# RetNet attention followed by a gated MLP on one core: the third group's two chunks taken jointly, the decay tables loaded at the start, one conversion step moved

## The chip, the cores and the metric

The kernel runs on one core of one Trainium2 chip. The metric is the device time of one execution in microseconds (us). TensorE does the matrix products; VectorE (DVE in the profile), ScalarE (ACT), GpSimd (POOL) and SyncE (SP) are the other engines. Each engine takes its instructions strictly in the order in which the program wrote them down. Transfers between HBM and SBUF are issued by an engine's instruction (here nearly all by SP and by POOL) and are carried by 16 shared DMA engines; SP's transfers go through one queue (q1 in the profile), POOL's through another (q0).

## The reference, cut to what matters

The first half is a linear attention with a decay per head, for 4 batches, 8 heads, 768 positions and a head dimension of 64. The second half takes its output as 3072 tokens of 512 features and sends them through a gated MLP with 2048 hidden units.

```python
for t in range(S):
    state = gamma[None, :, None, None] * state + np.einsum('bhd,bhe->bhde', k[:, :, t], v[:, :, t])
    y[:, :, t] = scale * np.einsum('bhd,bhde->bhe', q[:, :, t], state)
...
x = np.ascontiguousarray(attn_out.transpose(0, 2, 1, 3)).reshape(B * S, H * D)
h = x @ w_in
sp = np.maximum(h, 0.0) + np.log1p(np.exp(-np.abs(h)))
g = h * erf(sp)
return (g @ w_out).astype(np.float32)
```

The two weight matrices arrive as 64-bit floats, which the kernel turns into 32-bit ones by operations on their bits.

## The kernel before, in words

**Tiling.** The sequence is cut into chunks of 128 positions (`C`), 6 to a batch, 24 in all. Two chunks make a group of 256 tokens (`GT`), 12 groups in all. Chunks 0 to 3 (groups 0 and 1) are computed at the start by functions that take a whole chunk at once. From chunk 4 on a chunk is computed in two halves of 64 positions: `begin` makes the scores and the sums for the state on TensorE (lines 566 and 573), `states` masks the scores and adds up the running state on VectorE (582, 593), `results` makes the outputs on TensorE and copies them out on ScalarE (611, 622, 630), and `crossed_sums` adds the part that belongs to the other half (641). Before that a chunk needs its transposes, `T` = `ret_transpose` (453 on TensorE, the copies at 459 on ScalarE), and its scaled inputs, `scale_early` (line 746, eight small ScalarE operations each for the queries, argument 1, and for the values, argument 0).

**The first block.** After chunk 3 the loop over `ft` = 0 to 15 computes the hidden columns of groups 0 and 1, 128 columns a step, by plain 32-bit products (`hidden_of`, line 665). Each step has this order: the products of column tile `ft`; the weight conversions that are still wanted for a later tile (`need`); the entries of the table `during` for this `ft`; then `put_hidden(ft)`, which copies the finished tile out of PSUM on ScalarE (673) and stores it with two DMAs issued by POOL (675). There are two PSUM buffers for column tiles, so the products of tile `ft + 2` wait for the copy of tile `ft`. The table `during` is where the third group, chunks a = 4 and b = 5, is worked in between the column tiles. After the block the other groups run in periods of 8 units (`unit`, `pair_unit`) on split operands, and at the end the second MLP product follows.

**What sets the order of the work around the change.** It is all written out by hand: the list of calls ahead of the block, the table `during`, and the program's order on each queue. Nothing is planned by a scheduler. Four things lie on the queues that the change touches:

- `load(4)`, `load(5)` and their values (lines 136 and 143) are issued by SP, each when the conversion of weight piece 0 or 1 is done; SP's queue also carries the weight pieces (line 195) and the many small loads `kb` and `qb` (159).
- `load_pair(6)` is stepped by the `pair` entries of `during`. Its first step, at `ft` = 2, issues four transfers of 256 KB on POOL, the values and keys of chunks 6 and 7 (lines 143 and 153).
- `load_block_scales` issues 20 small transfers on POOL (by_b at line 389, four; kq_b at line 395, sixteen). They fill tables that `block_scales` (lines 401 to 405) reads at `ft` = 6 and that `prepare` needs from `ft` = 11.
- `next(weight_steps)` runs one step of the weight conversion, here of piece 0 (lines 230 to 265, VectorE with one ScalarE operation). `A` = `ret_add` adds a chunk's sums to the state on VectorE (525) and copies half of the outputs on ScalarE (518).

Of the kernel before, what the change touches and what calls it, by code (L numbers as in the profile page):

```python
# [32 lines left out]
def head(u, r):  # L33
    return u // 2 + u % 2 * 4 + 2 * r
# [15 lines left out]
def kernel(  # L50
# [34 lines left out]
    ps_r = ctx.enter_context(tc.tile_pool(name="ps_r", bufs=2, space=PSUM))  # L85
# [59 lines left out]
    def load_pair(j):  # L145

        b, c = divmod(j, NC)
        KNP[j] = b4("kn", [2, H, D])
        KB[j], QB[j] = (b4(name, [HP, 2 * C]) for name in ("kb", "qb"))
        for i in range(2):  # L150
            load_values(j + i, nc.gpsimd)
            KN[j + i], SLOT[j + i] = KNP[j][:, i], head
            nc.gpsimd.dma_start(KN[j + i], of_chunk(k, j + i))
        yield
        for to, src in ((KB[j], k), (QB[j], q)):
            for s, d in itertools.product(range(2), range(2)):
                part = slice((2 * s + d) * 32, (2 * s + d + 1) * 32)
                for u in range(HP):
                    nc.sync.dma_start(
                        to[part, u].rearrange("p (a d) -> p a d", d=32),  # L160
                        src[b, head(u, s), c * C : (c + 2) * C, d * 32 : (d + 1) * 32].rearrange(
                            "(a p) d -> p a d", p=32
                        ),
                    )
                yield
# [111 lines left out]
    def weights():  # L277

        parts = [(n, part) for n in range(2 * NPC) for part in (range(2) if n in HALVES else (None,))]
        for i, (n, part) in enumerate(parts):  # L280
            if n >= NPC or i < 3:
                exponents(n, part)
                yield
            yield from conversion(n, part, parts[i + 1] if i > 1 and i + 1 < EARLY else ())

    weight_steps = weights()
# [76 lines left out]
    def query_scale(c):  # L363
        nc.vector.reciprocal(kq_s[:, c, 1], kq_s[:, c, 0])
        nc.vector.tensor_scalar(kq_s[:, c, 1], kq_s[:, c, 1], unscale, None, op0=ALU.mult)
# [14 lines left out]
    def other_scales():  # L380
        query_scale(slice(2, NC))
# [5 lines left out]
    def load_block_scales():  # L387
        for s, i in itertools.product(range(2), range(2)):
            nc.gpsimd.dma_start(
                by_b[s * D : (s + 1) * D, 1, 2 * i : 2 * i + 2], decay_s[i * D : (i + 1) * D, s::2]  # L390
            )
        for s, d in itertools.product(range(2), range(2)):
            part = slice((2 * s + d) * 32, (2 * s + d + 1) * 32)
            for u in range(HP):
                nc.gpsimd.dma_start(
                    kq_b[part, 0, u, 0],
                    decay_k[:, head(u, s) : head(u, s) + 1].rearrange("(a p) h -> p (a h)", p=32),
                )
# [313 lines left out]
    def pair_unit(g, ft):  # L712
# [23 lines left out]
    Q_, V_, T, S_, M, O_, A = (  # L736
        scale_q, scale_v, ret_transpose, ret_scores, ret_mask, ret_out, ret_add
    )
# [3 lines left out]
    def scale_early(j, i):  # L742
        q = QN[j].rearrange("p (c g) d -> p c g d", c=2)
        for h in range(H):
            by, x = kq_s[:, j % NC, i, h : h + 1], q[:, h % 2, h // 2] if i else V[j][:, h]
            nc.scalar.activation(x, x, AF.Copy, scale=by)
# [5 lines left out]
    keep_warm(2)  # L752
    Q_(1)
    other_scales()
    S_(0)
    T(1, 0)
    T(1, 1)
# [13 lines left out]
    M(2)  # L771
    next(weight_steps)
    O_(1)
    next(weight_steps)
    T(3, 1)
    T(3, 0)
    scale_early(2, 0)
    A(1)
    next(weight_steps)
    O_(2, partial(S_, 3))  # L780
    M(3)
# [10 lines left out]
    def steps(s, n=1):  # L792
# [3 lines left out]
    pair = load_pair(JPC + 2)  # L796
    prep = prepare(JPC + 2)
    a, b = JPC, JPC + 1
    during = {
        1: [(load_block_scales,)],  # L800
        2: [(scale_early, a, 1), (steps, pair, 2)],
        3: [(scale_early, a, 0), (T, a, None, ("o2", "o3")), (steps, pair, 2)],
        4: [(begin, a, ps_r), (steps, pair, 2)],
        5: [(scale_early, b, 1), (states, a), (steps, pair, 2)],
        6: [(scale_early, b, 0), (results, a, ("o0", "o1")), (T, b, None, ("o2", "o3")), (steps, pair), (block_scales,)],
        7: [(crossed_sums, a), (begin, b, ps_r), (split_weights, 0)],
        8: [(states, b), (split_weights, 1)],
        9: [(results, b, ("o0", "o1"))],
        10: [(crossed_sums, b), (split_x, a, 2)],
        11: [(steps, prep, 3)],  # L810
        12: [(split_weights, 2), (steps, prep, 1)],
        13: [(steps, prep, 1)],
# [187 lines left out]
    for g in range(G2, NG + 1):  # L1000
        pair = load_pair(2 * g + 4) if 2 * g + 4 < NJ else iter(())
# [85 lines left out]
```

## Time and profile before

| | us |
|---|---|
| median of 3 runs | 612.78 |
| lowest and highest of them | 612.72, 613.2 |
| the profiled execution's own time | 613.15 |
| its span | 611.4 |
| TensorE busy in the span | 604.6 |
| VectorE, ScalarE, POOL busy | 459.8, 390.3, 132.5 |

How to read it: times in the trace count from the start of the span. Every answer groups instructions by the line of the kernel that wrote them. A row of the timeline gives the start, the length, the engine, the line, the operation and its tiles, and how many instructions were merged; in brackets stands the idle time of the engine ahead of it and what ended that. The engine's name with a q (SPq) marks the instruction that issues a transfer, not the transfer. The row of DMA in the page gives the share of the 16 DMA engines that was busy, in tenths, for 40 equal slices of the span. The chain is the run of work that ended last, followed back from the end. TensorE's granted clock is 1.0 in the whole span.

### The profile page before, as it was taken

To read this page: it belongs to the slowest core of one execution; us is meant where nothing else is said; L and a number is where in the kernel's file an instruction comes from. 1 tells how busy PE (TensorE), PEld (TensorE's weight loads), DVE (VectorE), ACT (ScalarE), POOL (GpSimd) and SP (SyncE) were. 2 spreads that over 40 slices of the span, in tenths; PEclk is the share of its full clock that TensorE was granted. 3 is DMA by queue.
4 is the path that set the end of the run, shared out by engine and by line. 5 is a ranking of instruction groups with operands and counts; after the bars stand their busy time and mean duration, and the time that the engine had idled before them with its cause. 6 is when DMAs were issued, how large, how long until landed. Compare 5 with 4: busy or idle time off the path is not lost.

```text
span 611.4 us, 13214 instructions
## 1 busy us (share of the span) xinstructions
PE 604.6 (99%) x5222; PEld 507.3 (83%) x5222; DVE 459.8 (75%) x581; ACT 390.3 (64%) x614; POOL 132.5 (22%) x228
## 2 busy tenths in 40 slices
PE   8999999999999999999999999999999999999997
PEld 7888889888888888888788988888888888888886
DVE  5899988886978679787768978686776768668640
ACT  3667446354453634345387699889789888988920
POOL 1087435443526535241112200000000000000000
PEclk9999999999999999999999999999999999999999
DMA  9999659977979998894645834325324333531300
GB/s 203 312 263 281 149 132 248 265 161 221 219 201 277 269 270 182 243 233 151 215 143 187 286 119 148 127 70 173 103 88 154 106 129 110 172 119 55 103 35 34
DMA packets 143949, 106.28 MB, mean 174 GB/s; under 512 B 103056, under 2 KB 123792, under 8 KB 143888
## 3 DMA queue, kind: packets, MB, share of 16 engines
q1 hardware_dynamic: 128160, 58.09, 37.4%
q0 software_dynamic: 15168, 47.21, 24.6%
q8 instruction: 41, 0.67, 0.5%
q10 hardware_dynamic: 560, 0.14, 0.1%
q14 instruction: 20, 0.16, 0.1%
HBM read 69.75 MB, written 35.65 MB: 172 GB/s over the span
## 4 chain that ended last, share of the span: by engine, by line
PE 96%; SPq 2%; DMA 1%; ACT 0%; DVE 0%; issue 0%; DVEq 0%
PE o L720 31%; PE o L905 21%; PE r L905 11%; PE hp L905 11%; PE hp L665 9%; PE o L693 3%; PE hp L566 1%; DMA raw<-in_moe_w_in_dram 1%; PE hp L720 1%; PE r L720 1%; PE r L566 1%; PE r L611 1%; SPq L136 1%; PE r L622 1%; PE r L573 1%; PE hp L611 1%
## 5 line engine op out<-in xcount | busy, mean ns | idle before, releaser
L720 PE MATMUL o<-x_hi,w_hi 128*128 128x512 f32 x272 | 108.0, 397 | 0.0
L322 ACT ACTIVATE h<-o 128x512 f32<-128x512 f32 x74 | 43.8, 595 | 98.7 <-PE o L720 89.3
L720 PE MATMUL o<-x_lo,w_lo 128*128 128x512 f32 x272 | 106.0, 390 | 0.0
L860 DVE TENSOR_TENSOR e<-hid,e 128x1024 f32<-128x1024 f32 x48 | 56.7, 1222 | 61.9 <-ACT e L850 61.9
L323 DVE SCALAR_TENSOR_TENSOR h<-o,h 128x512 f32<-128x512 f32 x74 | 50.5, 686 | 34.3 <-ACT h L322 24.8
L720 PE MATMUL o<-x_dif,w_dif 128*128 128x512 f32 x272 | 72.7, 389 | 0.0
L731 POOL DMA_DIRECT2D hids<-h x72 | 39.6, 550 | 131.2 <-DVE h L323 123.1
L316 DVE SCALAR_TENSOR_TENSOR g_dif<-g_hi,g_lo 128x1024 fp32r<-128x1024 f32 x48 | 58.8, 1226 | 3.3
L720 PEld LDWEIGHTS o<-x_hi,w_hi 128*128 128x128 f32 x272 | 51.0, 188 | 11.4
L720 PEld LDWEIGHTS o<-x_dif,w_dif 128*128 128x128 f32 x272 | 51.1, 188 | 10.6
L314 ACT ACTIVATE g_hi<-e 128x1024 fp32r<-128x1024 f32 x48 | 51.0, 1062 | 13.5 <-DVE e L860 11.6
L720 PEld LDWEIGHTS o<-x_lo,w_lo 128*128 128x128 f32 x272 | 51.1, 188 | 10.1
L315 DVE TENSOR_TENSOR g_lo<-e,g_hi 128x1024 fp32r<-128x1024 f32 x48 | 58.6, 1221 | 0.5
L665 PE MATMUL hp<-xT,w 128*128 128x256 f32 x256 | 57.2, 381 | 0.0
L665 PEld LDWEIGHTS hp<-xT,w 128*128 128x128 f32 x256 | 48.0, 190 | 6.6
L846 ACT ACTIVATE e<-hid 128x1024 f32<-128x1024 f32 x48 | 48.2, 1052 | 0.3
L850 ACT ACTIVATE e<-e 128x1024 f32<-128x1024 f32 x48 | 48.2, 1052 | 0.3
L905 PE MATMUL o<-w_hi,g_hi 128*128 128x512 f32 x120 | 46.7, 389 | 0.0
L905 PE MATMUL o<-w_lo,g_lo 128*128 128x512 f32 x120 | 46.7, 389 | 0.0
L905 PE MATMUL o<-w_dif,g_dif 128*128 128x512 f32 x120 | 46.7, 389 | 0.0
L550 ACT ACTIVATE v<-v,kq_s 128x64 f32<-128x64 f32 x144 | 35.6, 335 | 0.0
L846 ACT ACT_TABLE_LOAD x24 | 30.8, 1283 | 0.5
(201 smaller groups left out, 1265.6 us busy)
## 6 DMA issues: line engine op xcount, KB each, us to landing
hids<-h POOLq DMA_DIRECT2D x72, 256.0 KB, 4.1
hid<-hids SPq DMA_DIRECT2D x36, 512.0 KB, 4.6
raw<-in_moe_w_in_dram SPq DMA_DIRECT2D x32, 256.0 KB, 5.5
raw<-in_moe_w_out_dram POOLq DMA_DIRECT2D x32, 256.0 KB, 6.2
hid<-hid SPq DMA_DIRECT2D x12, 512.0 KB, 5.2
out_dram<-y SPq DMA_DIRECT2D x23, 256.0 KB, 2.1
kb<-in_k_dram SPq DMA_DIRECT2D x144, 32.0 KB, 2.8
v<-in_v_dram POOLq DMA_DIRECT2D x18, 256.0 KB, 6.0
```

The source lines that it names most:

```text
L314: nc.scalar.activation(hi, x, AF.Copy, scale=KEEP)
L315: nc.vector.tensor_tensor(lo, x, hi.bitcast(F32), op=ALU.subtract)
L316: nc.vector.scalar_tensor_tensor(dif, hi.bitcast(F32), Z, lo.bitcast(F32), op0=ALU.mult, op1=ALU.subtract)
L322: nc.scalar.activation(to, a, AF.Copy, scale=1 + 1 / Z)
L323: nc.vector.scalar_tensor_tensor(to, b, -1 / Z, to, op0=ALU.mult, op1=ALU.add)
L665: nc.tensor.matmul(HP_[ft][:, g], w[:, kk, ft % 2 * P : (ft % 2 + 1) * P], XC[g][:, kk], start=(kk == 0), stop=(kk == n_k - 1),)
L720: nc.tensor.matmul(to, W[n][i][:, kk * 2 * P + u * P : kk * 2 * P + (u + 1) * P], XR[i][:, at, kk], start=(kk == 0 and i == parts[0]), sto ...
L731: nc.gpsimd.dma_start(HID2[g][:, ft % 8], h)
L846: nc.scalar.activation(E[n], HID_[n], AF.Softplus)
L850: nc.scalar.activation(E[n], E[n], AF.Erf)
L860: nc.vector.tensor_tensor(E[n], HID_.pop(n), E[n], op=ALU.mult)
L905: nc.tensor.matmul(Y[g][t][x // 2], G[n][x][:, f, t * P : (t + 1) * P], W_OUT[ft // 2][x][:, ft % 2 * d_model : (ft % 2 + 1) * d_model], s ...
```

## The change

Three edits, all to the order of calls:

1. `load_block_scales()` leaves the table entry for `ft` = 1 and is called ahead of the first scores, right after `other_scales()`.
2. The second `next(weight_steps)` of the chunks' list moves from ahead of the transposes of chunk 3 to behind `A(1)`, the addition of chunk 1's sums to the state.
3. In `during`, the chunks a = 4 and b = 5 were staggered: a's `begin`, `states`, `results` stood at `ft` = 4, 5, 6 and b's at 7, 8, 9, with b's transposes at 6. Now b's scaling stands one step earlier (4 and 5), its transposes at 5 in the PSUM tiles o0 and o1, both `begin` at 6 (b's in o2 and o3), `states` at 7 and 8, both `results` at 9 and both `crossed_sums` at 10.

```diff
@@ the list of calls ahead of the block
     Q_(1)
     other_scales()
+    load_block_scales()
     S_(0)
...
     O_(1)
-    next(weight_steps)
     T(3, 1)
     T(3, 0)
     scale_early(2, 0)
     A(1)
+    next(weight_steps)
     next(weight_steps)
@@ the table during
-        1: [(load_block_scales,)],
         2: [(scale_early, a, 1), (steps, pair, 2)],
         3: [(scale_early, a, 0), (T, a, None, ("o2", "o3")), (steps, pair, 2)],
-        4: [(begin, a, ps_r), (steps, pair, 2)],
-        5: [(scale_early, b, 1), (states, a), (steps, pair, 2)],
-        6: [(scale_early, b, 0), (results, a, ("o0", "o1")), (T, b, None, ("o2", "o3")), (steps, pair), (block_scales,)],
-        7: [(crossed_sums, a), (begin, b, ps_r), (split_weights, 0)],
+        4: [(scale_early, b, 1), (steps, pair, 2)],
+        5: [(scale_early, b, 0), (T, b, None, ("o0", "o1")), (steps, pair, 2)],
+        6: [(begin, a, ps_r), (begin, b, None, ("o2", "o3")), (steps, pair), (block_scales,)],
+        7: [(states, a), (split_weights, 0)],
         8: [(states, b), (split_weights, 1)],
-        9: [(results, b, ("o0", "o1"))],
-        10: [(crossed_sums, b), (split_x, a, 2)],
+        9: [(results, a, ("o0", "o1")), (results, b)],
+        10: [(crossed_sums, a), (crossed_sums, b), (split_x, a, 2)],
```

The number and the shapes of all operations stay as they were.

## The prediction

> **What bounds the kernel now.** I read the page first, then TensorE's waits, then the chain and the queues' timelines between 30 and 60 us, and last the two transfer queues in two windows of ten microseconds. From the page:
>
> ```profile
> PE 604.6 (99%) x5222; PEld 507.3 (83%) x5222; DVE 459.8 (75%) x581; ACT 390.3 (64%) x614; POOL 132.5 (22%) x228
> DMA  9999659977979998894645834325324333531300
> ```
>
> TensorE is busy for 604.6 of 611.4 us, so a microsecond in which it newly waits is a microsecond on the end. The second line says that the 16 DMA engines are full in the first four slices, 0 to 61 us: exactly where the change lies. TensorE's waits in the whole span have four rows, 2.9 us together; one matters here:
>
> ```profile
> PE o L497 <- ACT kqT L459: 0.6, 1, 0.6
> ```
>
> So the most that ending waits can give is 0.6 us behind the start. The chain through the first block (start, length, what):
>
> ```profile
> 38.55 0.87 PE o L453 x8
> 39.42 3.46 PE hp L665 x16
> 42.88 0.62 PE r L566 x32
> 43.97 7.11 PE hp L665 x32
> ...
> 52.16 1.02 PE o L453 x8
> ...
> 84.48 0.47 PE o L566 x32
> ```
>
> A column tile is 16 products in 3.46 us. Two of them behind a run of small products take 7.11, not 6.92. A `begin` that follows a column tile starts with 0.62, one that follows another `begin` with 0.47. Changing between the kinds of product costs something.
>
> Now the queues: POOL, then SP (issues), then ScalarE.
>
> ```profile
> 32.09 2.39 POOL L389 DMA_DIRECT2D by_b<-decay_s_dram  x4
> 45.84 1.27 POOL L675 DMA_DIRECT2D hid<-h  x2
> 47.10 0.91 POOL L143 DMA_DIRECT2D v<-in_v_dram  x1
> ...
> 36.88 0.99 SPq L136 DMA_DIRECT2D kq<-in_q_dram  x2
> 37.91 1.06 SPq L136 DMA_DIRECT2D kq<-in_k_dram  x2
> 39.01 2.61 SPq L143 DMA_DIRECT2D v<-in_v_dram  x1
> ...
> 31.86 0.56 ACT L673 COPY h<-hp 128x512 f32<-128x512 f32 x1
> 47.53 2.01 ACT L746 ACTIVATE kq<-kq,kq_s 128x64 f32<-128x64 f32 x8
> ```
>
> The 20 table transfers hold POOL from 32.09 to 45.84, 13.7 us. Behind them stand tile 1's two stores, although ScalarE had copied that tile by 32.42, and then the four 256 KB loads for chunks 6 and 7. The SP rows are chunk 5's queries, keys and values. Last, what the two queues carried in 48 to 58 us, when POOL's stores and four loads were in flight, and in 34.6 to 44.6 us, when they were not:
>
> ```profile
> q0 software_dynamic: 513, 1.52, 61.5%
> q1 hardware_dynamic: 1871, 1.13, 47.6%
> ...
> q1 hardware_dynamic: 4880, 2.22, 98.7%
> q0 software_dynamic: 505, 0.12, 6.6%
> ```
>
> (packets, MB, share). With POOL's burst in flight SP's queue moved 1.13 MB in ten microseconds, without it 2.22.
>
> **The change part by part.**
>
> The conversion step behind the addition. At 17.32 and 17.78 VectorE runs the step's two operations (0.42 and 0.69 us); the addition follows at 18.39, and TensorE's line 497 starts at 18.95. With the addition first it ends near 17.8, and line 497 can start at 18.35, when the transposes ahead of it end. But the scores behind it (465, at 19.55) need ScalarE's copy, which ends at 19.40 as before. So 0.1 us is gained of at most 0.6; I take 0.1. The step itself still ends near 20.1, and its product starts at 22.18: covered by 2 us.
>
> The tables at the start. POOL is free from 6.69 (end of line 378) to 30.84, so 13.7 us of issuing costs no engine time. The transfers now share full DMA engines with chunks 2 and 3 and the first weight piece. They are 10 KB together; with the stores of tile 0 they made the 6.6% in the last window, at most 0.66 us. About half of them would go ahead of the last loads that TensorE waits for (chunk 3's keys, near 17.9). Between 0 and 0.66 us I take 0.1, nearest to their share of the bytes. At `ft` = 6 the tables' readers wait less (0.67 us on VectorE), which TensorE does not see.
>
> The chunks jointly. One `begin` and one `results` lose their own edges: the start of `begin` 0.62 - 0.47 = 0.15, the column tile behind it 7.11 - 6.92 = 0.19, the start of `results` 0.15 (line 611 has the same 0.62), and b's transposes, now behind a column tile, 1.02 - 0.87 = 0.15. Together -0.64 us. The moved VectorE work is covered: `states` of b ends at 60.9 in the trace and both `results` are wanted near 63; both `crossed_sums` stand at `ft` = 10, and their reader, the first unit, starts at 90.94.
>
> What POOL does with the free time is the large term. Its next entries move forward to where ScalarE releases them: tile 1's stores from 45.84 to 32.4, the four loads from 47.10 to about 33.7, all by 13.4 us. So the burst of 48 to 58 comes to 34.6 to 44.6, the time in which SP's queue brings chunk 5. SP then carries 2.22 - 1.13 = 1.09 MB less, and at 0.222 MB per us it needs 1.09 / 0.222 = 4.9 us more. Queries of chunk 5 landed 5.6 us after their issue, the second at 37.37 + 5.6 = 43.0; keys 5.9 after, at 44.4; values 6.5 after, at 45.5. They come to 47.9, 49.3 and 50.4.
>
> Edit 3 wants them sooner: b's transposes started at 52.16, 7.8 us behind the keys. Now they start at 38.55 + 0.87 + 2 x 3.46 = 46.34, and tile 6 should start at 47.2. ScalarE stands at `scale_early(b, 1)` until 47.9, works 2.0 us, and behind it in its queue waits the copy of tile 4 (0.57), which frees the buffer that tile 6 writes: 47.9 + 0.1 + 2.0 + 0.6 = 50.6. TensorE waits 50.6 - 47.2 = 3.4 us, first for the keys (49.3), then for the scaled queries and the buffer. Nothing later takes it back, since TensorE has no other wait to absorb it. Next in line is tile 7, which needs tile 5's copy: ScalarE's 50.6 + 1.15 (an exponent step) + 2.0 + 1.04 + 0.57 = 55.4 against TensorE's 50.6 + 3.46 + 1.56 = 55.6; just in time. The bounds: no stall if the delay is under 1.5 us; at the other end a weight transfer issued at 49.2, inside the burst, took 11.2 us where the median is 5.4: a delay of 5.8 and a stall of 4.3. The windows stand between; I take 3.4.
>
> The sum: -0.1 + 0.1 - 0.64 + 3.4 = +2.8 us on the profiled execution's 613.15 us (span and what lies around it), 615.9. That execution lies 0.37 above the median of 612.78, so on the median's scale the forecast is 615.6.
>
> The Trainium skill, "DMA: Bandwidth & Descriptors", section "Queues, rings and completion order", says that a DMA engine takes turns between its queues by whole packets. By strict turns one of POOL's packets would pass for each of SP's; the window has 513 against 1871, so the trace does not bear that out, at least as its packets are counted; the sum by the rule is the last rival below.
>
> **The rivals.**
>
> *The loads stay hidden.* If the DMA engines take the early burst in the pauses that the sharing leaves, chunk 5 is late by under 1.5 us and the edges alone remain: -0.64, so 612.1. For it: the engines were at about 0.85 from 38 to 40 us. Against it: they are at nine tenths elsewhere, and 1.4 MB more does not fit.
>
> *Half hidden.* A delay between 1.5 and 3.3 us gives a stall of 0 to 1.8: 612.1 to 613.9, in the middle 613.0. For it: without 256-byte packets in the way SP's queue may regain more than 0.222 MB per us.
>
> *The other side: the addition sets the pace.* If line 497 was held by the addition alone and what follows it runs 0.6 us sooner all the way, and no load is late, the time is 613.15 - 0.64 - 0.63 - 0.37 = 611.5. It decides if chunk 5's keys land by 46.3. Against it: the scores' copy ends at 19.40 whatever VectorE does.
>
> *The stall grows.* A long wait could lower TensorE's granted clock, 1.0 in every slice before; half a tile's time to a whole tile's at half speed costs 1.7 to 3.5 us, 617.3 to 619.1. Or SP's queue gets only packet for packet: 513 of its packets of 0.6 KB are 0.31 MB, 1.91 MB less, 8.6 us of delay, a stall of 7.1, and 619.2. Against the first: the wait is broken by the keys' transposes after 3 us. The Trainium skill, "TensorE: Matmul & The Clock Gate", section "What's actually happening", puts the fall to half clock at an idle window of about 3.4 us; no run here shows it. The second of these is what the rule of turns would do.
>
> **How the numbers follow.** The late chunk 5 as worked out: 0.57, by itself 614.2 to 616.5 (stall 2.0 to 4.3). Hidden 0.15, half hidden 0.14, faster 0.06, grown 0.08. A measurement of this kernel can tell about 0.2%, 1.2 us. Faster is the third rival, 0.06; the same are the first two, 0.29; slower is the rest, 0.65. The range leaves out the third rival's time and the grown stalls, 0.14 together, and reaches from just under the hidden case to above the likeliest one's 616.5: 612.0 to 617.0.
>
> **What would show it.** Right: POOL's loads of chunks 6 and 7 at about 33.7; chunk 5's transfers landing about ten microseconds after their issue; ScalarE idle ahead of line 746; TensorE waits of some 3 us in all ahead of lines 453 and 665 between 46 and 51; 0.62 then 0.47 in one run of `begin`; line 497 near 18.35. Wrong: POOL's loads still after 45, or no TensorE row over 1 us in that stretch, or new waits elsewhere (at the start, on the first weight piece, or at 63 on `states`).

## The result and the profile after

The changed kernel took 615.88 us (median of six, 615.51 to 616.88) against 612.82 of the kernel before in the same comparison (612.63 to 613.2). The ratio is 1.0052, with a 95% interval of 1.0039 to 1.0065: slower by 3.1 us, where 2.8 was forecast (615.6 on the median's scale). The profiled execution of the changed kernel is its slowest, 616.88 us with a span of 615.2.

First the waits of TensorE in the kernel after (who waited for what, us in total, times, longest):

```profile
PE o L453 <- DMA kq<-in_k_dram: 2.2, 1, 2.2
PE o L417 <- POOL ident masks.py:199: 1.5, 1, 1.5
```

The 2.2 us are new: the transposes wait for keys. No other row is above 0.3 us; the 0.6 at line 497 is gone. The timeline of TensorE shows the place, and that of ScalarE, POOL and SP the causes (start, length, engine, line; the idle time ahead in brackets):

```profile
39.95 7.07 PE L665 MATMUL hp<-xT,w 128*128 128x256 f32 x32
49.27 1.55 PE L453 MATMUL o<-ident,kq 128*128 128x128 f32 x8 [2.24 <-DMA kq<-in_k_dram]
50.95 3.72 PE L665 MATMUL hp<-xT,w 128*128 128x256 f32 x16
```

```profile
48.06 0.35 ACT L746 ACTIVATE kq<-kq,kq_s 128x64 f32<-128x64 f32 x1 [3.49 <-DMA kq<-in_q_dram]
48.65 1.78 ACT L746 ACTIVATE kq<-kq,kq_s 128x64 f32<-128x64 f32 x7 [0.25 <-DMA kq<-in_q_dram]
50.34 0.56 ACT L673 COPY h<-hp 128x512 f32<-128x512 f32 x1
```

```profile
33.42 1.07 POOL L675 DMA_DIRECT2D hid<-h  x2 [0.77 <-ACT h L673]
34.48 0.91 POOL L143 DMA_DIRECT2D v<-in_v_dram  x1
```

```profile
37.69 1.19 SPq L136 DMA_DIRECT2D kq<-in_q_dram  x2
38.93 3.60 SPq L136 DMA_DIRECT2D kq<-in_k_dram  x2
```

POOL's first 256 KB load starts at 34.48 instead of 47.10. Chunk 5's queries, issued at 37.69, let ScalarE start only at 48.06, after an idle time of 3.49 us; the copy of tile 4 stands behind that scaling, and tile 6 starts at 50.95. The transfer queues in the same ten microseconds as in the prediction, 34.6 to 44.6 us (packets, MB, share of 16 engines; then issues, KB each, us to landing):

```profile
q0 software_dynamic: 519, 1.60, 55.6%
q1 hardware_dynamic: 1948, 1.35, 50.5%
...
kq<-in_q_dram SPq DMA_DIRECT2D x2, 128.0 KB, 10.3
kq<-in_k_dram SPq DMA_DIRECT2D x2, 128.0 KB, 9.0
```

SP's queue moved 1.35 MB where it moved 2.22 before, and the queries took 10.3 us from issue to landing instead of 5.6.

To see where the time went, I cut every span in three: up to the first column tile's products, from there to the first unit (the block), and the rest.

| run | change against the kernel before | first tile at | block | rest | median, and ratio with interval |
|---|---|---|---|---|---|
| before | | 22.18 | 68.69 | 520.53 | 612.79 to 612.96 in the four comparisons |
| after | all three edits | 22.88 | 71.34 | 520.98 | 615.88, 1.0052 (1.0039 to 1.0065) |
| e1 | edits 2 and 3, tables back at `ft` = 1 | 22.09 | 68.49 | 520.72 | 613.14, 1.0003 (0.9994 to 1.0012) |
| e2 | edit 1 alone | 22.84 | 68.68 | 520.68 | 613.99, 1.0018 (1.0009 to 1.0027) |
| e3 | edit 2 alone | 21.90 | 68.69 | 520.71 | 612.96, 1.0002 (0.9993 to 1.0011) |
| e4 | all, the pair's loads held | 23.18 | 68.02 | 520.60 | 613.35, 1.0008 (1.0000 to 1.0017) |
| e5 | edits 2 and 3, tables spread, loads held | 21.99 | 68.91 | 520.50 | 612.95, 1.0003 (0.9994 to 1.0012) |
| e6 | all, half of the pair's loads held | 22.92 | 68.02 | 520.56 | 613.30, 1.0009 (1.0000 to 1.0017) |
| e7 | before, 20 other transfers at the start | 21.83 | 68.68 | 520.49 | 613.02, 1.0004 (0.9995 to 1.0012) |
| e8 | all, joint chunks one tile later | 22.93 | 68.79 | 520.58 | 613.92, 1.0020 (1.0011 to 1.0029) |
| e9 | edits 2 and 3, tables by copies, loads held | 22.17 | 68.02 | 520.61 | 612.29, 0.9987 (0.9978 to 0.9995) |
| e10 | all, tables by copies | 22.30 | 72.45 | 520.75 | 617.03, 1.0054 (1.0040 to 1.0068) |
| e11 | as e10, one of four loads held | 22.09 | 69.65 | 520.66 | 614.21, 1.0020 (1.0011 to 1.0028) |

The first three columns are one profiled execution each. The rest scatters over 0.5 us, so no effect of the change can be told behind the first 95 us. The 3.8 us between the two profiled spans are 0.7 at the start, 2.65 in the block and 0.45 in the rest, which is scatter.

### The profile page after: what moved, and what is told of

The parts are those of the page before. It is cut to its first block, busy times and chain, and to the rows that moved or that the text cites. A ratio compares the mean times of both kernels' runs of the same rounds, so it can differ in the third digit from the quotient of the medians.

```text
span 615.2 us, 13216 instructions
## 1 busy us (share of the span) xinstructions
PE 606.5 (99%) x5222; PEld 508.7 (83%) x5222; DVE 459.9 (75%) x581; ACT 390.9 (64%) x614; POOL 132.9 (22%) x228
## 4 chain that ended last, share of the span: by engine, by line
PE 91%; DMA 5%; SPq 3%; DVE 1%; ACT 0%; issue 0%; DVEq 0%
PE o L720 31%; PE o L905 21%; PE hp L905 11%; PE r L905 11%; PE hp L665 6%; DMA raw<-in_moe_w_in_dram 3%; PE o L693 3%; DMA kq<-in_q_dram 2%; SPq L136 1%; PE hp L566 1%; PE r L611 1%; PE hp L720 1%; PE r L720 1%; PE r L622 1%; SPq L195 1%; PE r L566 1%
## 5 line engine op out<-in xcount | busy, mean ns | idle before, releaser
L323 DVE SCALAR_TENSOR_TENSOR h<-o,h 128x512 f32<-128x512 f32 x74 | 50.6, 687 | 35.1 <-ACT h L322 27.6
```

The lines of the kernel that those rows point to most:

```text
L323: nc.vector.scalar_tensor_tensor(to, b, -1 / Z, to, op0=ALU.mult, op1=ALU.add)
```

## The experiments

### e1: the tables back at their old place

```diff
     other_scales()
-    load_block_scales()
     S_(0)
...
+        1: [(load_block_scales,)],
         2: [(scale_early, a, 1), (steps, pair, 2)],
```

> The changed kernel with the table loads put back to ft = 1, so that POOL's stores of tile 1 and its four 256 KB loads wait behind them again. The joint taking of the chunks and the moved conversion step stay. My theory (the early burst on POOL's queue makes chunk 5 late): no TensorE wait at b's transposes, chunk 5's queries land under 6 us after their issue, and the saved edges alone remain, about 612.2 us. Rival 1 (the joint order by itself wants chunk 5 too early): the wait of 2 to 3 us at b's transposes stays and the time is 615 to 616 us. Rival 2 (the tables at the start delay everything that follows): the first column tile starts near 22.2 instead of 22.9 us and 0.7 us of the loss goes away through that alone.

The stall at b's transposes is gone: the joint order alone is not too early, and rival 1 falls. But the time is 613.14, not 612.2. The block is 68.49, and its chain (start, length) shows another wait:

```profile
48.00 1.68 ACT v L746 x7
49.73 0.21 POOL hid L675
49.94 0.82 issue
50.76 8.39 DMA hid<-h
59.25 0.60 ACT h L673
59.89 3.72 PE hp L665 x16
```

ScalarE's tile copy at 59.25 waits for a store on POOL's queue to land; the copies go through six buffers, and these are taken as long as the stores are not done. That store stood behind the table loads and the pair's four loads until 49.73, and then took 8.39 us to land, with those four loads in flight. In the kernel before that wait existed too (2.59 us on ScalarE at 58.93) and TensorE did not see it. With the joint order the products come sooner and it does: 0.20 us of waiting, and the three column tiles from 52.51 on take 11.03 us where they take 10.56 in a run without the wait (e9), which is the block's whole loss against 68.02. So the first edit is not idle: it takes this wait away, at a price of its own. How much of the wait the table loads make alone, with the pair's loads held and the tables left at `ft` = 1, was not run.

### e2: the tables at the start, nothing else

```diff
     other_scales()
+    load_block_scales()
     S_(0)
...
-        1: [(load_block_scales,)],
```

> The kernel before with the table loads at the start and nothing else changed; the staggered chunks stay. My theory: chunk 5 lands about ten microseconds after its issue, as in the changed kernel, but b's transposes are wanted only near 52 us, so TensorE does not wait: 612.8 us, within 0.6. Rival 1 (the early tables themselves cost time at the start): first column tile 0.7 us later, 613.5 us. Rival 2 (the late loads stall the block in any order): a TensorE wait over 1 us between 45 and 60 us and 614 us or more.

The block is unchanged, 68.68 against 68.69: chunk 5's queries landed 9.8 us after their issue, nearly as late as in the changed kernel, but with the staggered chunks that cost TensorE nothing. But the first tile starts at 22.84, 0.66 us later than in the kernel before, and the time is 613.99, 1.05 us above it: rival 1 holds, and my theory of "no cost" falls. The waits of TensorE name the place:

```profile
PE r L453 <- DMA kq<-in_k_dram: 0.8, 2, 0.6
```

The keys of chunk 3 are late. The five runs with the table loads at the start all have this wait, 0.2 to 1.2 us, and the eight others have none. In 7 to 17 us SP's queue moved 2.17 MB instead of 2.30.

### e3: the conversion step alone

```diff
     O_(1)
-    next(weight_steps)
     T(3, 1)
...
     A(1)
+    next(weight_steps)
     next(weight_steps)
```

> The kernel before with the second conversion step moved behind the addition of chunk 1 and nothing else. My theory: line 497 starts earlier, but the scores behind it wait for ScalarE's copy, so 0.1 us is gained: 612.7 us. Rival (the addition sets the pace of the start): line 497 and all that follows comes 0.6 us sooner, 612.2 us.

612.96 against 612.94: no difference that can be told. The wait at line 497 has left TensorE's list, as expected. The wait for ScalarE's copy that was expected behind it, at line 465, can't be seen in this profile: its 0.5 us at that line are at 7.65 and 10.57 us, where the kernel before has 0.6 as well. Three other runs with the moved step have it (e9, e10 and e11), here e9, where the line has number 466:

```profile
19.43 0.37 PE L466 MATMUL r<-kqT 64*128 64x128 f32 x1 [0.52 <-ACT kqT L460]
```

The first tile came at 21.90 in the profiled execution, 0.28 earlier; that is about the scatter of this point between runs with the same start (21.83 to 22.30).

### e4: the pair's loads held

```diff
-        2: [(scale_early, a, 1), (steps, pair, 2)],
-        3: [(scale_early, a, 0), (T, a, None, ("o2", "o3")), (steps, pair, 2)],
-        4: [(scale_early, b, 1), (steps, pair, 2)],
-        5: [(scale_early, b, 0), (T, b, None, ("o0", "o1")), (steps, pair, 2)],
+        2: [(scale_early, a, 1)],
+        3: [(scale_early, a, 0), (T, a, None, ("o2", "o3"))],
+        4: [(scale_early, b, 1)],
+        5: [(scale_early, b, 0), (T, b, None, ("o0", "o1")), (steps, pair, 7)],
```

> The changed kernel, tables at the start, with the steps of load_pair held until ft = 5 and 6, so that POOL's four 256 KB loads come after chunk 5's transfers. POOL's stores of the tiles stay early. My theory: no wait at b's transposes, the saved edges remain, 612.2 us. Rival 1 (the tables at the start delay the loads): still 613 us or more. Rival 2 (the joint order is too early by itself): 615 to 616 us.

The wait is gone and the block is 68.02, shorter than before by 0.67: the edges. The first tile is at 23.18, the latest of all, so the time is 613.35. Rival 1 holds for the start and falls for chunk 5. The stall belongs to the pair's loads, the loss at the start to the tables. From 34.6 to 44.6 us the queues carried:

```profile
q1 hardware_dynamic: 5361, 2.31, 89.5%
q0 software_dynamic: 267, 0.71, 18.8%
```

Beside POOL's stores, 0.71 MB, SP's queue moved no less than in the kernel before (2.31 MB against 2.22, there beside the table loads), and chunk 5's queries landed 4.8 us after their issue. What it would move beside nothing at all was not run.

### e5: the tables spread over the block

```diff
+        0: [(steps, tables)],
+        1: [(steps, tables)],
-        2: [(scale_early, a, 1), (steps, pair, 2)],
+        2: [(scale_early, a, 1), (steps, tables)],
...
```

Each step issues four of the 20 loads; the pair's loads are held as in e4.

> The changed kernel with the joint chunks and the moved step, but with POOL's 20 table loads four at a time at ft = 0 to 4 and the pair's four 256 KB loads held to ft = 5. My theory now has three terms: tables at the start +0.7 us (gone here, since they are not at the start), the saved edges -0.67 (kept), the early burst +3.3 (gone), and in the run with the tables back a new stall of 0.5 us, because the tile stores stood behind all 20 loads (mostly gone here). So 612.2 us, first column tile near 22.1, block 68.0 to 68.2 us. Rival: 20 loads between the stores still hold the six buffers of the tile copies up, a wait at line 665 on ScalarE stays and the time is 612.8 or more.

The rival's signs came: the first tile is at 21.99, but a wait of 0.4 us of the column tiles for ScalarE's copy stays, the block is 68.91 and the gain is gone. Its reason is another, though. No copy on ScalarE waits for a store here. VectorE waits, for the last table loads, which POOL issues only at 44.42; first its row, then TensorE's (lines 406 and 669 here are 402 and 665 of the kernel before):

```profile
51.87 0.25 DVE L406 RECIPROCAL kq_b<-kq_b 128x16 f32<-128x16 f32 x1 [3.20 <-DMA kq_b<-decay_k_dram]
...
69.10 3.07 PE L669 MATMUL hp<-xT,w 128*128 128x256 f32 x13 [0.38 <-ACT h L677]
```

The reciprocal of the tables stands at 51.87 instead of 48.67 (e9), and all of VectorE's work behind it, which stands in the order of the program, is some 3 us late. An exponent step of ScalarE waits for it until 66.76 (63.46 in e9), the tile copy behind that starts at 68.43, and TensorE waits for the copy. From 65.00 to the next scores five column tiles take 18.35 us, where they take 17.47 in e9: that is the block's whole loss against 68.02. So the tables, spread as they are here, come too late for their reader at `ft` = 6; fewer tiles or a later reader were not tried.

### e6: half of the pair's loads early

```diff
             nc.gpsimd.dma_start(KN[j + i], of_chunk(k, j + i))
-        yield
+            yield
...
-        2: [(scale_early, a, 1), (steps, pair, 2)],
+        2: [(scale_early, a, 1), (steps, pair)],
```

> The changed kernel with two of the pair's four loads (0.5 MB, chunk 6) at ft = 2 as before and the other two held to ft = 5. My theory, in which chunk 5 is late by the bytes that POOL puts in front of it: the burst is 1.0 MB instead of 1.5, the delay 3.3 us instead of 4.9, the stall 1.8 instead of 3.4, 614.3 us. Rival (any early load of the pair costs the whole stall, through an issue order or a buffer): 615.9. Rival (half the burst fits into the pauses): no stall, 613.3.

No stall at all: block 68.02. The second rival fits, but not for its reason. SP's queue moved 1.82 MB in the ten microseconds, halfway between 2.31 (held) and 1.35 (all four), so the delay does go by the pair's bytes. My mistake was to count the stores' 0.5 MB in the burst as well; beside the stores alone (e4) SP's queue moved no less. The queries landed 7.1 us after their issue, 1.5 later than at first, which is just the slack worked out in the prediction.

### e7: twenty other transfers at the start

```diff
     other_scales()
+    load_unused()
...
+    def load_unused():
+        for i in range(20):
+            part = slice(i % 4 * 32, (i % 4 + 1) * 32)
+            nc.gpsimd.dma_start(
+                kq_b[part, 1, i // 4 % 4, 1 + i // 16], decay_k[part, i % 2 * 4 : i % 2 * 4 + 4]
+            )
```

> The kernel before, its tables still at ft = 1, with 20 further transfers of 512 bytes on POOL at the same early place, each as 32 elements of 16 bytes; the tables' own transfers are 128 elements of 4 bytes. They fill places that are overwritten later. If the loss at the start goes by the number of transfers: first column tile near 22.9 us, 613.6 us or more. If it goes by the number of elements: a quarter of the loss, first column tile near 22.35, 613.1 us. If it was chance: 22.1.

The first tile came at 21.83, no wait for chunk 3's keys is left, and SP's queue moved 2.29 MB in 7 to 17 us, as without the transfers (2.30). So neither the number of POOL's transfers nor their bytes make the start late; nor do the packets as the profile counts them, 461 on POOL's queue in that window against 380 in e2. The median is 0.23 us above the kernel before, which by itself can be told neither from nothing nor from a quarter of the loss. What differs is the form: 128 elements of 4 bytes, each apart from the next in HBM, against 32 elements of 16 bytes. Whether the number of elements or their spacing costs the time was not tried.

### e8: the joint chunks one tile later

```diff
-        4: [(scale_early, b, 1), (steps, pair, 2)],
-        5: [(scale_early, b, 0), (T, b, None, ("o0", "o1")), (steps, pair, 2)],
-        6: [(begin, a, ps_r), (begin, b, None, ("o2", "o3")), (steps, pair), (block_scales,)],
+        4: [(steps, pair, 2)],
+        5: [(scale_early, b, 1), (steps, pair, 2)],
+        6: [(scale_early, b, 0), (T, b, None, ("o0", "o1")), (steps, pair), (block_scales,)],
+        7: [(begin, a, ps_r), (begin, b, None, ("o2", "o3")), (split_weights, 0)],
...
```

> The changed kernel, tables at the start and pair's loads early, with everything of the joint chunks from b's scaling on one column tile later (3.46 us). My theory: chunk 5 lands as late as in the changed kernel, near 49, but is wanted at 50.4 instead of 47; a stall of 0 to 0.4 us, so tables +0.7 and edges -0.67 remain: 613.0 us, within 0.4. Rival (the early burst holds up more than chunk 5, for instance the tile stores or the weight pieces): 614 us or more.

The wait for chunk 5's keys is gone with the same early burst, so the stall is the meeting of a late load and an early need. But the time is 613.92, outside my 0.4, and the block 68.79: nearest to the rival. The early burst also holds the weight pieces up. On VectorE the exponents of a weight piece wait, and b's `states` come late for `results`; first VectorE's row, then TensorE's:

```profile
54.33 0.69 DVE L230 TENSOR_SCALAR power<-raw 128x1024 uint32<-128x1024 uint32 x1 [1.89 <-DMA raw<-in_moe_w_in_dram]
...
69.31 0.46 PE L611 MATMUL r<-kqT,state 64*64 64x64 f32 x16 [0.31 <-DVE state L593]
```

The outputs at `ft` = 10 take 2.56 us around this wait, from 67.60 to the next column tile at 70.16, where they take 2.02 in e9. That is 0.54 of the 0.77 us over 68.02; the rest lies in smaller pieces.

### e9, e10, e11: the tables without transfers

All three make the tables by 18 small POOL copies, at the early place, from the decays that already lie in SBUF:

```diff
-            nc.gpsimd.dma_start(
-                by_b[s * D : (s + 1) * D, 1, 2 * i : 2 * i + 2], decay_s[i * D : (i + 1) * D, s::2]
-            )
...
+        for s, d, x in itertools.product(range(2), range(2), range(4)):
+            part = slice((2 * s + d) * 32, (2 * s + d + 1) * 32)
+            nc.gpsimd.tensor_copy(
+                kq_b[part, 0, :, 0, x].rearrange("p (i j) -> p i j", j=2),
+                d_k[x * 32 : (x + 1) * 32].rearrange("p (j s i) -> p s i j", s=2, i=2)[:, s],
+            )
```

> The changed kernel with the pair's loads held to ft = 5 and with no table transfers at all: POOL makes the two tables at the same early place by 18 small copies out of the decays that already lie in SBUF. My theory: no loss at the start (first column tile near 22.1 us), POOL's queue free so that the tile stores are never late, chunk 5 on time: the saved edges alone remain, block 68.0 us, 612.1 us, faster than the kernel before. Rival (the edges are given back elsewhere, or the start is late for another reason): 612.7 us or more.

With the pair's loads held, nothing of the loss is left: start 22.17, block 68.02, 612.29 us, a ratio of 0.9987 (0.9978 to 0.9995) to the kernel before. It is the fastest version found, 0.7 us below the kernel before. POOL's rows at the start:

```profile
6.54 0.42 POOL L390 COPY by_b<-d_s 64x4 f32<-64x4 f32 x2
7.02 4.83 POOL L396 COPY kq_b<-d_k 32x4 f32<-32x4 f32 x16
```

> The changed kernel with the table transfers replaced by the same 18 copies and nothing else; the pair's loads come at ft = 2. This separates the two losses. My theory: start 22.1 us, the wait at b's transposes stays whole, block 71.3 us, 615.3 us. Rival (the table transfers at the start also make chunk 5 late): block under 70 us, 614 us or less.

With all four loads early the stall stays, 2.03 us at the keys and 0.7 behind them, with no table transfer in the program: no part of the tables' transfers in it can be told. The block is 72.45, longer than expected, and this has a cause of its own. First the rows of TensorE, then busy time by engine in two windows, with the granted clock as the third number from the end:

```profile
48.47 1.36 PE L454 MATMUL o<-ident,kq 128*128 128x128 f32 x8 [2.03 <-DMA kq<-in_k_dram]
49.91 5.29 PE L666 MATMUL hp<-xT,w 128*128 128x256 f32 x16
```

```profile
50.00:52.00 2.00, 2.00 (x5) 1.65 (x6) 1.54 (x2) 2.00 (x6) 1.08 (x2) 0.50 0.94 304
52.00:54.00 2.00, 2.00 (x8) 1.63 (x8) 0.00 (x0) 2.00 (x7) 0.00 (x0) 0.72 1.06 286
```

The column tile behind the wait took 5.29 us instead of 3.62, at a granted clock of 0.50 up to 52 us and of 0.72 from there to 54. With 2.76 us of waiting and 1.67 of slow products the block comes out exactly: 68.02 + 2.76 + 1.67 = 72.45. That is the prediction's case of the growing stall. By the times and the mean clocks it comes in four of the six executions (616.89 to 617.48 us, mean clock 0.997) and not in the other two (614.60 and 615.21, clock 0.999 and 1.0). Those two are near the 615.3 of the theory, which has no change of the clock in it.

> As the run before, with three of the pair's four loads at ft = 2 and the fourth held to ft = 5. With four loads early the queries of chunk 5 landed 10.3 us after their issue and with two 7.1, so 8.7 is expected here. My theory (delay by the bytes, stall where the delay passes the slack): with two loads the slack was just used up, so a stall of about 1.6 us, block 69.7 us, 613.8 us. Rival (the stall comes only with the last load, chunk 7's keys): no stall, 612.1 us.

Block 69.65 and 614.21 us: as expected within 0.4. The queries landed 9.0 us after their issue. With no, two, three and four of the loads early SP's queue moved 2.31, 1.82, 1.64 and 1.35 MB, the queries landed 4.8, 7.1, 9.0 and 10.3 us after their issue, and the block was 68.02, 68.02, 69.65 and 71.34 (e4, e6, e11, after): the delay grows with every load, the stall only beyond the slack.

## Why the prediction was right, and where it was not

**What bounds.** Right. TensorE is still busy for 99% of the span, and its new wait lengthened the span.

**The early burst and the stall, +3.4.** Right in mechanism and place; in size it fits the profiled execution better than the medians. POOL's loads came at 34.48 (33.7 forecast); the queries landed 4.7 us later after their issue (4.9), tile 6 started at 50.95 (50.6; the start, 0.7 us late, is in the 50.95), and the block grew by 71.34 - 68.02 = 3.3 us over the version in which only the loads are held (e4). That execution is the slowest of the six, though, 1.0 us above their median. By medians the changed kernel is 3.06 us above the kernel before and e4 is 0.41 above it, so holding the loads is worth 2.65 us. The delay of 4.9 us came nearer than its own working: SP's queue lost 2.22 - 1.35 = 0.87 MB and not 1.09, and by the same division that is 3.9 us. That 4.7 was measured is in part luck. And the 1.09 MB was read as stores and loads together; by e4 and e6 the loads do it.

**The edges, -0.64.** Right: 68.69 - 68.02 = 0.67, the same in e4, e6 and e9; by medians e9 is 0.67 below the kernel before.

**The tables at the start, +0.1 of 0 to 0.66.** Wrong. The term of the sum that was mis-sized is this one. Five runs with the table loads at the start have their first tile at 22.84 to 23.18, mean 22.95; the eight others at 21.83 to 22.30, mean 22.07. The cost is 0.9 us (1.05 by e2's median), nine times the value taken and above the upper bound. The step that failed was to bound it by the transfers' share of the DMA engines' time in a window of the block; the queue that shares the engines lost more than that share. In e2 the table transfers take 2.9% of the engines from 7 to 17 us, 0.29 us, and SP's queue lost 0.13 MB, at 0.23 MB per us some 0.6 us; where the rest of the 0.9 lies is open. The wait that it makes, 0.25 us in the changed kernel for chunk 3's keys, is a new wait at the start, which the prediction had named among the signs of being wrong.

**The moved step, -0.1.** It can't be told from nothing (e3). The wait it removes is gone; the one named behind it, for ScalarE's copy, is seen in e9, e10 and e11 (0.52, 0.63 and 0.49 us), not in e3's own profile.

**What POOL's queue did before.** Not in the sum, and it should have been: in the joint order POOL's late stores, behind the table loads and the pair's loads, cost 0.5 us through the tile copies' buffers (e1). Undoing the first edit alone takes the stall away, but this wait then eats the edges: 613.14, no faster than the kernel before.

**The sum.** +2.8 was forecast, +3.1 came. By medians, each against the kernel before of its own comparison, the terms are 1.05 (tables, e2), -0.67 (edges, e9) and 2.65 (stall): 3.03 against the 3.06 measured. So the tables were taken 0.95 us too low and the stall 0.75 too high, and the two errors nearly cancel. The mechanism of the large term was right; that the number lies within 0.3 us is in part luck.

**The rivals.** The hidden loads and the half-hidden case needed fewer loads than four: e6 and e11 are those cases. The addition did not set the pace (e3). The rule of turns by packets, from the Trainium skill, "DMA: Bandwidth & Descriptors", section "Queues, rings and completion order", did not give the size: SP's queue passed 1948 packets beside POOL's 519. The falling clock did not happen in the changed kernel (mean clock 0.999 or 1.0 in all six executions), but it did in e10, where the slow column tile cost 1.67 us.

## What to carry to other kernels

Taking work off a queue releases what stood behind it, and the released transfers may meet others that are wanted soon: work out when each queue's next entries will then start, and what is in flight at that time. Moving a consumer earlier spends slack; add up the slack that both edits of one change spend, since either alone cost nothing in the block here. Taking transfers out was worth more here than moving them: the tables by copies from SBUF, with the loads held, gave the only version faster than the kernel before.

## What the runs showed of the hardware that was not expected

Twenty transfers of 512 bytes on POOL's queue, as 4-byte elements that lie apart, made TensorE wait for loads of SP's queue and cost about 1 us (e2: 1.05 us by the medians); twenty of the same size as 16-byte elements cost nothing that can be told (e7: 0.23 us, within the interval).

A wait of TensorE that was broken after 2.03 us by four transposes still brought the granted clock down to 0.50. By the windows 50 to 52 and 52 to 54 us it lost 1.0 and 0.56 us, so it stood at half for some 3.1 us there, and the 0.96 in the four microseconds before adds some 0.3 us to that. In the changed kernel a wait of 2.24 us, broken in the same way, left the clock at 1.0 in the profiled execution. The Trainium skill, "TensorE: Matmul & The Clock Gate", section "What's actually happening", gives free-running windows of about 3.4 us; the length of the fall, and that it comes in some executions of one program and not in others, agree with that. A wait as long as a whole idle window, as the Trainium skill puts it, was not needed here.
